# Batch 0 keeps 36 more score tiles and reads them back turned; queries, u and weight steps are placed anew

## The chip, the cores and the metric

One core of one Trainium2 chip. The metric is the device time of one execution in microseconds: the median of three runs, 2047.68 us for the kernel before (2046.53 to 2050.74). Engines: TensorE (PE) does the matmuls, VectorE (DVE), ScalarE (ACT) and GpSimd (POOL) work elementwise, SyncE (SP) issues the DMAs.

## What is computed

Two stages, in float32. Cut to what matters:

```python
# u, v: (4, 3008, 256); z: (4, 3008, 64)
scores = (1 / 3008) * z @ z.T              # per batch, symmetric
out = u * ((np.maximum(scores, 0) ** 2) @ v)
x = out.reshape(12032, 256)
xn = x / sqrt(mean(x * x, -1) + 1e-6) * rms_g
g, val = xn @ w_gate, xn @ w_val           # 256 -> 1536
y = (g * sigmoid(g) * val) @ w_out         # 1536 -> 256
```

The scores are symmetric: the score of query q and key k is that of query k and key q. The kernel uses this to compute some score tiles once and to read them back transposed.

## The kernel before

**Numbers.** Every float32 operand is split into a high and a low part for TensorE, and a product is three matmuls (high x high, low x high, high x low). A score needs two, since z stands in its array as high and low at once.

**Stages.** The 4 batches are cut into 3 pairs of query chunks (2 x 512 queries), so there are 12 pairs p, three for each batch. Each pair has an attention phase A(p) and a phase M(p) for the second stage. The attention phases of batch 0, p = 0, 1, 2, run first, one after the other (called phase 0, 1 and 2 here); then M(0), A(3), M(1), A(4) and so on. In the trace phase 0 ends at about 92 us, phase 1 at about 190 us, and the first matmuls of M(0) come at 276 us.

**A phase.** It has 24 slots, one for each tile of 128 keys, in the sequence that `order(p)` gives. In slot i the program writes: the scores of tile i + 2 for both query chunks (`emit_s`: two matmuls L415, L416 each; relu on ACT, L423; then either the product with itself on DVE, L430, or, for every second one, two squares on ACT, L450 and L451); the split of tile i + 1 into H on ACT (L453 or L450) and L on DVE (L456); a hook with whatever was planned for this slot; and the 12 matmuls of tile i with v (`emit_av`, L501, L502, L506). So a slot is 16 matmuls. At the end of a phase `emit_gate` multiplies the four sums by u (L531) and sends them to DRAM.

**Kept and turned tiles.** Where `keeps(b, c, kc)` says so, the tile of query chunk c and key chunk kc > c is also copied as 16-bit halves (`halves`, L475 on DVE or L477 on ACT, two of five on DVE; three buffers) and stored in DRAM (`kept`, L481). A later pair for which the chunks change places loads it with a transposing DMA (`load_turned`, L394), one load for two key tiles and one query chunk, into one of six buffers with the tag T. Such a slot needs no score matmuls, no relu and no product; H and L are made from the loaded tile. The later batches keep every such tile. Batch 0 keeps only those of chunk 4 against 5: four.

**Weights.** During phases 0, 1 and 2 the weights are decoded from 64-bit halves and combined: loads into the same six T buffers (`wraw`, L152), four short steps on DVE, one on ACT, then pieces of 128 columns on POOL (L140 for the projections, L201 and L202 for w_out). A combination is split by ACT (`wohi`, L231) and POOL (`wolo`) and stored in DRAM by SP (L236) one slot later. `at_step(g, ...)` places each at slot g % 24 of phase g // 24. The norm of pair 0 runs in slots 5 to 19 of phase 1 and in phase 2.

**Order.** The program's order is kept on each engine (`manual_schedule`): an engine runs its instructions as written and waits at each for what it needs. SP issues all DMAs in one order too, so a DMA that waits holds up those behind it. The queries of phases 1 and 2 (`prep_mov`, L292) go through the two buffers `raw`, which v, z and two of the four u tiles use as well; a split on DVE (L296, L301) makes mh and ml of them in slots 21 and 22 of the phase before. The u tiles are loaded (`load_u`, L521) in slots 21 (one) and 23 (three).

Of the kernel before, what the change touches and what calls it, by code (L numbers as in the profile page):

```python
# [8 lines left out]
F32 = mybir.dt.float32  # L9
# [21 lines left out]
def kernel(  # L31
# [176 lines left out]
    def prep_proj(j, pool, tags):  # L208
# [62 lines left out]
        "batch": ["mh0", "ml0", "mh1", "ml1", "raw", "raw"],  # L271
        "queries": ["raw"],
    }
# [7 lines left out]
    def prep_mov(p, k):  # L281
# [5 lines left out]
        def load():  # L287
            if p >= LAG:
                raw = tiles["raw"] = work.tile([P, CH], F32, tag=("u", "ws")[k], name="raw")
            else:  # L290
                raw = tiles["raw"] = new_raw("queries" if p else "start")
            nc.sync.dma_start(out=raw[:, :n], in_=zT2[:, t0 + k * CH:t0 + k * CH + n])  # L292
# [79 lines left out]
    def order(p):  # L372
        b, c0 = where(p)[:2]
        if p == 0:
            return list(range(NK))
        first = list(range(4 * (c0 + 1), min(4 * (c0 + 2), NK)))
        last = list(range(4 * c0, 4 * c0 + 4))
        return first + [k for k in range(NK) if k not in first and k not in last] + last

    def keeps(b, c, kc):  # L380
        return b > 0 or c >= 4

# [527 lines left out]
    for p in range(NPAIR):  # L910
# [4 lines left out]
        for i in range(0, NK, 2):  # L915
            for k in range(2):
                if is_turned(p, i, k):
                    go = lambda p=p, i=i, k=k: load_turned(p, i, k)
                    if i < 8 and p >= LAG:
                        at(("M", p - LAG), 3 * (NF - 2 if i < 6 else NF - 1) + 1, go)  # L920
                    else:
                        at(ph, max(i - 7, 0), go)
        if p >= LAG - 1:
            for f in range(ahead(p - LAG + 1)):
                at(ph, NK - 3 + f, lambda p=p, f=f: load_unit(p - LAG + 1, f))
        at(ph, NK - 3, lambda p=p: load_u(p, [(0, 0)]))
        at(ph, NK - 1, lambda p=p: load_u(p, [(0, 1), (1, 0), (1, 1)]))

# [73 lines left out]
    for p in range(1, NPAIR):  # L1002

        for k in range(2):
# [5 lines left out]
            else:  # L1010
                at(("A", p - 1), NK - (5 if p == 1 else 10), load)
                at(("A", p - 1), NK - 3 + k, split)
# [31 lines left out]

    for j, steps, end in ((0, (4, 8, 12, 16), 20), (1, (21, 25, 29, 33), 36), (2, (37, 40, 43, 47), 50)):
        parts, ends = prep_proj(j, moving, tags_w[j])
        for g, part in zip(steps, parts):
            plan_part(part, g)
        for k, fns in zip((0, 1, 2, 3, 5, 7, 8, 10, 12), ends):
            for fn in fns:  # L1050
                at_step(end + k, fn)
    for f, g in zip(range(0, 8, 2), (50, 55, 59, 63)):
        plan_part(prep_wout(f), g)
# [74 lines left out]
```

## Time and profile before

| | |
|---|---|
| median of 3 runs | 2047.68 us |
| the profiled execution, device time | 2047.41 us |
| its span, first to last instruction | 2045.6 us |
| PE busy | 2023.9 us (99%), 8976 matmuls |
| DVE, ACT, POOL busy | 1610.9, 1426.3, 225.8 us |
| granted TensorE clock, mean | 0.998 |

A matmul's busy time is modelled and its neighbours overlap, so a PE that is busy for 99% need not run at its best pace; how many matmuls a stretch holds says more. A short wait of PE and the lower clock after it show as fewer matmuls in a stretch. Rows of the trace name an engine, the line, the operation and the tiles (out<-in). A wait is put down to the instruction that ended it.

### The profile page before, as it was taken

The page shows a single profiled execution, that of the slowest core. Times are in us where ns is not written, and L with a number is a line of the kernel's source. Part 1 is how long each engine was busy: PE and PEld are TensorE (multiplying, and loading weights), DVE is VectorE, ACT ScalarE, POOL GpSimd, SP SyncE. Part 2 cuts the span into 40 slices and gives each one's busy share as a digit, 9 for nine tenths or more (in the row PEclk, how much of TensorE's full clock was granted, in tenths as well). Part 3 has the DMA queues.
Part 4 walks back from the last instruction along what each step waited for, and adds up shares of the span by engine and source line. Part 5 has one row for each costly group of instructions (what it writes and reads, how often), then busy time and mean ns, then how long its engine had stood idle before and what let it go on. Part 6 is the DMA issues. An engine that isn't in the chain of part 4 may idle for free.

```text
span 2045.6 us, 27209 instructions
## 1 busy us (share of the span) xinstructions
PE 2023.9 (99%) x8976; PEld 1680.8 (82%) x8976; DVE 1610.9 (79%) x2657; ACT 1426.3 (70%) x2578; POOL 225.8 (11%) x376
## 2 busy tenths in 40 slices
PE   9998999999999999999999999999999999999999
PEld 7786888888888888888888888888888888888887
DVE  7888988988877768797776876878777777777765
ACT  8787977886675666697567574679656757566665
POOL 0355815100000000400000000220000000000000
PEclk9999999999999999999999999999999999999999
DMA  3345375264555496346465459725544747734342
GB/s 110 108 125 160 108 240 183 104 211 148 134 157 183 141 212 213 103 163 210 136 144 173 147 147 203 234 89 174 196 134 128 212 136 169 190 126 157 118 147 91
DMA packets 320654, 320.50 MB, mean 157 GB/s; under 512 B 196736, under 2 KB 235776, under 8 KB 320512
## 3 DMA queue, kind: packets, MB, share of 16 engines
q1 hardware_dynamic: 320512, 318.77, 51.7%
q8 instruction: 70, 1.15, 0.2%
q14 instruction: 72, 0.59, 0.1%
HBM read 190.78 MB, written 81.79 MB: 133 GB/s over the span
## 4 chain that ended last, share of the span: by engine, by line
PE 88%; DVE 4%; ACT 3%; issue 2%; POOL 2%; DMA 1%; SPq 0%; DVEq 0%; ACTq 0%; POOLq 0%
PE po L501 11%; PE po L502 11%; PE po L506 11%; PE ps L700 10%; PE ps L701 10%; PE ps L702 10%; PE py L728 6%; PE py L729 6%; PE py L732 6%; PE ps L416 4%; PE ps L415 4%; POOL w L140 1%; POOL wolo L140 1%; ACT s L707 1%; ACT r L423 1%
## 5 line engine op out<-in xcount | busy, mean ns | idle before, releaser
L501 PE MATMUL po<-H,vh 128*128 128x512 f32 (+1 forms) x1152 | 447.8, 389 | 4.5 <-DVE u L531 2.1
L502 PE MATMUL po<-H,vl 128*128 128x512 f32 (+1 forms) x1152 | 445.4, 387 | 0.0
L707 ACT COPY s<-ps 128x512 f32<-128x512 f32 (+1 forms) x432 | 249.5, 578 | 217.5 <-PE ps L702 217.5
L700 PE MATMUL ps<-xh,wu 128*128 128x512 f32 (+1 forms) x1008 | 392.0, 389 | 1.9 <-ACT s L707 1.8
L701 PE MATMUL ps<-xh,wu 128*128 128x512 f32 (+1 forms) x1008 | 388.7, 386 | 0.0
L702 PE MATMUL ps<-xl,wu 128*128 128x512 f32 (+1 forms) x1008 | 388.6, 385 | 0.0
L506 PE MATMUL po<-L,vh 128*128 128x512 f32 (+1 forms) x1104 | 336.8, 386 | 3.5 <-DVE L L456 3.0
L712 ACT CAST hH<-s 128x512 fp32r<-128x512 f32 (+1 forms) x288 | 176.6, 613 | 203.9 <-DVE s L794 200.1
L430 DVE TENSOR_TENSOR r<-ps,r 128x512 f32<-128x512 f32 (+1 forms) x327 | 213.9, 681 | 99.7 <-ACT r L423 98.7
L423 ACT ACTIVATE r<-ps 128x512 f32<-128x512 f32 (+1 forms) x392 | 214.8, 593 | 110.1 <-PE ps L416 96.0
L717 DVE TENSOR_TENSOR hL<-s,hH 128x512 fp32r<-128x512 f32 (+1 forms) x288 | 201.0, 698 | 104.4 <-ACT hH L712 91.1
L501 PEld LDWEIGHTS po<-H,vh 128*128 128x128 f32 x1152 | 216.8, 188 | 52.7 <-DVE H L460 2.7
L456 DVE TENSOR_TENSOR L<-r,H 128x512 fp32r<-128x512 f32 x368 | 248.0, 706 | 14.4 <-ACT r L451 14.3
L502 PEld LDWEIGHTS po<-H,vl 128*128 128x128 f32 x1152 | 217.0, 188 | 40.5
L506 PEld LDWEIGHTS po<-L,vh 128*128 128x128 f32 x1104 | 206.7, 188 | 46.1 <-DVE L L456 7.4
L700 PEld LDWEIGHTS ps<-xh,wu 128*128 128x128 f32 x1008 | 189.1, 188 | 47.0 <-ACT s L707 10.0
L728 PE MATMUL py<-hH,woh 128*128 128x512 f32 (+1 forms) x576 | 222.2, 386 | 0.1
L729 PE MATMUL py<-hH,wol 128*128 128x512 f32 (+1 forms) x576 | 222.0, 385 | 0.0
L702 PEld LDWEIGHTS ps<-xl,wu 128*128 128x128 f32 x1008 | 189.2, 188 | 36.1
L701 PEld LDWEIGHTS ps<-xh,wu 128*128 128x128 f32 x1008 | 189.2, 188 | 34.9 <-DMA wu<-wc 0.4
L453 ACT CAST H<-r 128x512 fp32r<-128x512 f32 (+1 forms) x327 | 191.5, 622 | 3.3 <-DVE r L430 3.2
L362 POOL TENSOR_TENSOR vl<-raw,vh 128x128 fp32r<-128x128 f32 x144 | 81.4, 603 | 940.2 <-ACT vh L351 937.6
(85 smaller groups left out, 2912.4 us busy)
## 6 DMA issues: line engine op xcount, KB each, us to landing
wu<-wc SPq DMA_DIRECT2D x288, 448.0 KB, 4.0
kept<-halves SPq DMA_DIRECT2D x168, 256.0 KB, 2.0
raw<-in_v SPq DMA_DIRECT2D x44, 256.0 KB, 2.9
u<-in_uT SPq DMA_DIRECT2D x40, 256.0 KB, 4.6
xg<-u SPq DMA_DIRECT2D x40, 256.0 KB, 2.3
raw<-in_zT SPq DMA_DIRECT2D x38, 256.0 KB, 4.5
ux<-xg SPq DMA_DIRECT2D x16, 512.0 KB, 4.8
out_T<-y SPq DMA_DIRECT2D x32, 256.0 KB, 2.2
```

The lines of the kernel that those rows point to most:

```text
L423: nc.scalar.activation(a[:, :n], ps[:, :n], AF.Relu)
L430: nc.vector.tensor_tensor(a[:, :n], ps[:, :n], a[:, :n], op=ALU.mult)
L456: nc.vector.tensor_tensor(lo[:, :n], a[:, :n], f32(hi[:, :n]), op=ALU.subtract)
L501: nc.tensor.matmul(po[d][:, :n], wh[:, j, ds], hi[:, :n], start=(i == 0), stop=False)
L502: nc.tensor.matmul(po[d][:, :n], wl[:, j, ds], hi[:, :n], start=False, stop=(ends and lo is None))
L506: nc.tensor.matmul(po[d][:, :n], wh[:, j, ds], lo[:, :n], start=False, stop=ends)
L700: nc.tensor.matmul(ps[:, :n], wh[:, o, :], xh[:, :n], start=start, stop=False, skip_group_check=True)
L701: nc.tensor.matmul(ps[:, :n], wl[:, o, :], xh[:, :n], start=False, stop=False, skip_group_check=True)
L702: nc.tensor.matmul(ps[:, :n], wh[:, o, :], xl[:, :n], start=False, stop=stop, skip_group_check=True)
L707: nc.scalar.copy(s, ps[:, :self.n])
L728: nc.tensor.matmul(acc[h, d][:, :n], woh[:, f, ds], hi[:, :n], start=(f == 0), stop=False)
L729: nc.tensor.matmul(acc[h, d][:, :n], wol[:, f, ds], hi[:, :n], start=False, stop=False)
```

## The change

It does six things. (1) `keeps` lets batch 0 keep more: chunk 0 against 2 and 3, chunk 1 against 4 and 5, chunks 2 and 3 against every later one, 36 tiles more (16 made in phase 0, 20 in phase 1; 12 read in phase 1, 24 in phase 2). (2) In batch 0 `order` takes new and turned key tiles by turns, two and two. (3) Turned tiles of the first phases are loaded five slots ahead, not seven. (4) The queries of phases 1 and 2 go to buffers of their own, q0 and q1, and those of phase 1 are loaded in slot 14, not 19, of phase 0. (5) In every phase the u tiles are loaded two in slot 21 and two in slot 22. (6) The steps of the second and third part of the projection weights and of w_out get other numbers.

```diff
@@ -269,7 +269,6 @@
     raws = {
         "start": ["raw", "xl4", "raw", "xl5", "xl6"],
         "batch": ["mh0", "ml0", "mh1", "ml1", "raw", "raw"],
-        "queries": ["raw"],
     }
 
     def new_raw(what):
@@ -285,10 +284,11 @@
         tiles = {}
 
         def load():
-            if p >= LAG:
-                raw = tiles["raw"] = work.tile([P, CH], F32, tag=("u", "ws")[k], name="raw")
+            if p:
+                tag = ("u", "ws")[k] if p >= LAG else f"q{k}"
+                raw = tiles["raw"] = work.tile([P, CH], F32, tag=tag, name="raw")
             else:
-                raw = tiles["raw"] = new_raw("queries" if p else "start")
+                raw = tiles["raw"] = new_raw("start")
             nc.sync.dma_start(out=raw[:, :n], in_=zT2[:, t0 + k * CH:t0 + k * CH + n])
 
         def high():
@@ -375,10 +375,20 @@
             return list(range(NK))
         first = list(range(4 * (c0 + 1), min(4 * (c0 + 2), NK)))
         last = list(range(4 * c0, 4 * c0 + 4))
-        return first + [k for k in range(NK) if k not in first and k not in last] + last
+        rest = [k for k in range(NK) if k not in first and k not in last]
+        if b == 0:
+
+            new, old = [], []
+            for k in rest:
+                (old if k // 4 < c0 and keeps(b, k // 4, c0) else new).append(k)
+            rest = []
+            while new or old:
+                rest += new[:2] + old[:2]
+                del new[:2], old[:2]
+        return first + rest + last
 
     def keeps(b, c, kc):
-        return b > 0 or c >= 4
+        return b > 0 or c >= 2 or kc // 2 == c + 1
 
     def is_turned(p, i, k):
         b, c0 = where(p)[:2]
@@ -919,12 +929,12 @@
                     if i < 8 and p >= LAG:
                         at(("M", p - LAG), 3 * (NF - 2 if i < 6 else NF - 1) + 1, go)
                     else:
-                        at(ph, max(i - 7, 0), go)
+                        at(ph, max(i - (7 if p >= LAG else 5), 0), go)
         if p >= LAG - 1:
             for f in range(ahead(p - LAG + 1)):
                 at(ph, NK - 3 + f, lambda p=p, f=f: load_unit(p - LAG + 1, f))
-        at(ph, NK - 3, lambda p=p: load_u(p, [(0, 0)]))
-        at(ph, NK - 1, lambda p=p: load_u(p, [(0, 1), (1, 0), (1, 1)]))
+        at(ph, NK - 3, lambda p=p: load_u(p, [(0, 0), (0, 1)]))
+        at(ph, NK - 2, lambda p=p: load_u(p, [(1, 0), (1, 1)]))
 
     def plan_splits(p, phase, slots):
         jobs_ = split_jobs_at(p)
@@ -1008,7 +1018,7 @@
                 at(m.phase, 3 * 9 + 1 + k, load)
                 at(m.phase, 3 * 10 + 2 + k, split)
             else:
-                at(("A", p - 1), NK - (5 if p == 1 else 10), load)
+                at(("A", p - 1), NK - 10, load)
                 at(("A", p - 1), NK - 3 + k, split)
 
 
@@ -1042,14 +1052,14 @@
         for k, (_, _, _, fn) in zip((0, 0, 0, 1, 1, 2, 2, 2), ops):
             at_step(g + k, fn)
 
-    for j, steps, end in ((0, (4, 8, 12, 16), 20), (1, (21, 25, 29, 33), 36), (2, (37, 40, 43, 47), 50)):
+    for j, steps, end in ((0, (4, 8, 12, 16), 20), (1, (18, 26, 29, 33), 36), (2, (36, 39, 42, 50), 52)):
         parts, ends = prep_proj(j, moving, tags_w[j])
         for g, part in zip(steps, parts):
             plan_part(part, g)
         for k, fns in zip((0, 1, 2, 3, 5, 7, 8, 10, 12), ends):
             for fn in fns:
                 at_step(end + k, fn)
-    for f, g in zip(range(0, 8, 2), (50, 55, 59, 63)):
+    for f, g in zip(range(0, 8, 2), (53, 56, 60, 64)):
         plan_part(prep_wout(f), g)
 
     with tc.manual_schedule():
```

What this does to the order on three engines' queues follows.

SP at the end of phase 0; raw<-in_zT of L292 are the queries, u the u tiles, wc the combined weights. Before:

```order
L152 DMA wraw<-in_w_gate 128x1024
L292 DMA raw<-in_zT 128x512 x2
L521 DMA u<-in_uT 128x512
L236 DMA wc_80<-wohi 128x4x128
L236 DMA wc_80<-wolo 128x4x128
L152 DMA wraw<-in_w_gate 128x1024
L236 DMA wc_80<-wohi 128x4x128
L236 DMA wc_80<-wolo 128x4x128
L521 DMA u<-in_uT 128x512 x3
```

After:

```order
L292 DMA raw<-in_zT 128x512 x2
L491 DMA kept_804<-halves 128x1024
L343 DMA raw<-in_v 128x2x256
L152 DMA wraw<-in_w_gate 128x1024
L491 DMA kept_804<-halves 128x1024 x2
L345 DMA raw<-in_v 128x256
L347 DMA raw<-in_v 64x256 x2
L491 DMA kept_804<-halves 128x1024
L491 DMA kept_982<-halves 128x1024 x3
L531 DMA u<-in_uT 128x512 x2
L236 DMA wc_80<-wohi 128x4x128
L236 DMA wc_80<-wolo 128x4x128
```

The queries now stand ahead of the last loads of v, and two u tiles ahead of the first weight store; stores of kept tiles have come in between.

ACT in phase 1 at slots 15 and 16 (L433 is the relu, L463 and L460 make H, L461 squares, L487 copies the halves). Before:

```order
L423 ACTIVATE r<-ps 128x512 x2
L453 CAST H<-r 128x512
L450 ACTIVATE H<-r 128x512
L451 ACTIVATE r<-r 128x512
L423 ACTIVATE r<-ps 128x512 x2
L450 ACTIVATE H<-r 128x512
L451 ACTIVATE r<-r 128x512
L453 CAST H<-r 128x512
L157 ACTIVATE w_1846<-wraw 128x512
```

After:

```order
L433 ACTIVATE r<-ps 128x512 x2
L463 CAST H<-r 128x512
L460 ACTIVATE H<-r 128x512
L461 ACTIVATE r<-r 128x512
L487 COPY halves<-r 128x1024 x2
L157 ACTIVATE w_1873<-wraw 128x512
L433 ACTIVATE r<-ps 128x512 x2
L460 ACTIVATE H<-r 128x512
L461 ACTIVATE r<-r 128x512
L463 CAST H<-r 128x512
L487 COPY halves<-r 128x1024
```

Each slot has got one or two copies of twice the width behind its tiles.

SP in the second half of phase 2 (T<-kept are the transposing loads, wraw<-in_w_out the last weights). Before:

```order
L152 DMA wraw<-in_w_out 128x2x512
L236 DMA wc_82<-wohi 128x4x128
L236 DMA wc_82<-wolo 128x4x128
L236 DMA wc_82<-wohi 128x4x128
L236 DMA wc_82<-wolo 128x4x128
L152 DMA wraw<-in_w_out 128x2x512
L236 DMA wc_82<-wohi 128x4x128
L236 DMA wc_82<-wolo 128x4x128
L394 DMA_TRANSPOSE T<-kept_2184 128x2x896
L236 DMA wc_82<-wohi 128x4x128
L236 DMA wc_82<-wolo 128x4x128
L394 DMA_TRANSPOSE T<-kept_2184 128x2x896
```

After:

```order
L404 DMA_TRANSPOSE T<-kept_1654 128x2x1024
L404 DMA_TRANSPOSE T<-kept_1855 128x2x896
L404 DMA_TRANSPOSE T<-kept_1654 128x2x1024
L404 DMA_TRANSPOSE T<-kept_1855 128x2x896
L152 DMA wraw<-in_w_out 128x2x512
L236 DMA wc_82<-wohi 128x4x128
L236 DMA wc_82<-wolo 128x4x128
L404 DMA_TRANSPOSE T<-kept_1657 128x2x1024
L404 DMA_TRANSPOSE T<-kept_1858 128x2x896
L236 DMA wc_82<-wohi 128x4x128
L236 DMA wc_82<-wolo 128x4x128
L236 DMA wc_82<-wohi 128x4x128
```

Pairs of transposing loads now stand among the stores of wolo, which wait for POOL, and share the T buffers with the loads of w_out.

## Rows read from the trace of the kernel before

**Rows 1.** Stretches (us): PE, PEld, DVE, ACT, POOL busy (count), clock, DMA share, GB/s

```profile
25.00:87.00 62.00, 62.00 (x275) 51.32 (x275) 51.90 (x85) 54.82 (x102) 11.63 (x20) 1.00 0.22 70
87.00:105.00 18.00, 15.36 (x58) 11.53 (x57) 17.10 (x27) 11.12 (x21) 10.62 (x16) 0.91 0.67 214
105.00:168.00 63.00, 63.00 (x280) 52.20 (x279) 54.32 (x84) 55.91 (x104) 37.60 (x63) 1.00 0.42 127
168.00:203.00 35.00, 27.38 (x107) 20.43 (x107) 30.47 (x53) 22.50 (x41) 20.64 (x34) 0.95 0.54 162
203.00:262.00 59.00, 58.30 (x264) 48.82 (x263) 55.72 (x80) 53.98 (x103) 49.22 (x73) 1.00 0.42 115
276.00:2045.00 1769.00, 1762.22 (x7853) 1467.94 (x7852) 1370.99 (x2284) 1196.47 (x2153) 90.03 (x160) 1.00 0.54 161
```

**Rows 2.** Waits of PE, 0 to 260 us: total us, times, longest

```profile
PE ps L415 <- DVE mh L296: 4.4, 3, 2.1
PE po L506 <- DVE L L456: 3.0, 4, 1.3
PE po L501 <- DVE u L531: 2.1, 2, 1.6
```

**Rows 3.** Time line of SP: start, us, line, operation, tiles, count

```profile
73.73 13.90 SPq L292 DMA_DIRECT2D raw<-in_zT  x2
...
192.72 0.36 SPq L236 DMA_DIRECT2D wc<-wolo  x1
193.18 1.43 SPq L521 DMA_DIRECT2D u<-in_uT  x3
```

**Rows 4.** Waits of SP's queue, 0 to 260 us: total us, times, longest

```profile
SPq L236 <- POOL wolo L140: 62.7, 21, 7.7
...
SPq L292 <- DVE vl L357: 25.3, 2, 13.1
```

**Rows 5.** DMA issues: count, KB each, median us to landing

```profile
u<-in_uT SPq DMA_DIRECT2D x40, 256.0 KB, 4.6
...
T<-kept SPq DMA_TRANSPOSE x92, 4.8
```

**Rows 6.** Groups of ACT, 25 to 75 us: busy us, mean ns, idle before

```profile
L423 ACT ACTIVATE r<-ps 128x512 f32<-128x512 f32 x28 | 15.2, 594 | 4.3 <-PE ps L416 4.3
...
L453 ACT CAST H<-r 128x512 fp32r<-128x512 f32 x14 | 8.6, 614 | 0.0
```

**Rows 7.** The copies of kept tiles, whole run: ns min/median/max

```profile
L477 ACT COPY halves<-r x118: 1028/1056/1093, 195.1 to 1716.9; 128x1024 uint16<-128x1024 uint16 x102, 64x1024 uint16<-64x1024 uint16 x16
L475 DVE COPY halves<-r x66: 684/690/698, 377.9 to 1602.7; 128x1024 uint16<-128x1024 uint16 x66
```

**Rows 8.** Stretches with POOL nearly idle and full, columns as in rows 1

```profile
25.00:75.00 50.00, 50.00 (x222) 41.38 (x222) 41.32 (x68) 45.28 (x85) 7.46 (x12) 1.00 0.26 82
216.00:260.00 44.00, 43.30 (x195) 35.83 (x194) 43.00 (x61) 39.13 (x76) 42.73 (x61) 1.00 0.44 119
```

**Rows 9.** DVE's L and product in those two stretches: ns min/median/max

```profile
L456 DVE TENSOR_TENSOR L<-r,H x26: 681/686/804, 27.4 to 71.5; 128x512 fp32r<-128x512 f32 x26
L456 DVE TENSOR_TENSOR L<-r,H x26: 667/838/1020, 216.7 to 259.6; 128x512 fp32r<-128x512 f32 x13, 128x448 fp32r<-128x448 f32 x13
L430 DVE TENSOR_TENSOR r<-ps,r x14: 682/684/693, 25.7 to 74.7; 128x512 f32<-128x512 f32 x14
L430 DVE TENSOR_TENSOR r<-ps,r x13: 611/648/679, 216.1 to 257.5; 128x512 f32<-128x512 f32 x7, 128x448 f32<-128x448 f32 x6
```

**Rows 10.** SP's issues of transposing loads, whole run: ns min/median/max

```profile
L394 SPq DMA_TRANSPOSE T<-kept x92: 1311/2100/5577, 252.7 to 1749.8; - x92
```

## The prediction

> **What bounds the kernel now.** I read the table of stages first [rows 1]. From 276 us to the end TensorE holds 7853 matmuls in 1769 us and stands still for under 7 us, so nothing is to be had there. Batch 0's first phase is as dense: 275 matmuls in 62.00 us, 0.2255 us each, with ACT busy 54.82 and DVE 51.90. What is open lies around the phases' ends. At 0.2255 us the stretch 87 to 105 us has room for 79.8 matmuls and holds 58: 4.9 us lost. The stretch 168 to 203 us has room for 155.2 and holds 107: 10.9 us lost. From 203 to 262 us there are 264, half of them 448 columns wide (0.028 us shorter): 59.0 - 264 x 0.2255 + 132 x 0.028 = 3.2 us lost. Together 19.0 us. The clock shows in two of them: 0.91 over 18 us and 0.95 over 35 us are 3.2 and 3.5 us at the lower of the two levels (1.2 GHz), after TensorE had stood still; at half pace that is 1.6 and 1.8 us of the losses.
>
> The waits of TensorE name the releasers [rows 2]: the scaled queries mh of the next phase (4.4 us), L of a tile (3.0), the gate on u (2.1). The queue of SP says why they are late [rows 3]. The queries' two loads span 13.90 us, since the second waits for a buffer; three u loads stand behind a store of wolo that goes out at 192.72, once POOL has the data. SP's own waits have both: 13.1 us at most for the buffer, 7.7 for POOL [rows 4].
>
> **The change, part by part.**
>
> *Score matmuls.* 36 tiles fewer to multiply (12 in phase 1, 24 in phase 2), two matmuls each: 24 and 48, of which 24 are 448 wide. 48 x 0.2255 + 24 x 0.2255 x 448/512 = 15.6 us less on TensorE, and TensorE is what runs through [rows 1]. Gain 15.6.
>
> *Queries and u.* The queries get q0 and q1, free in phase 0 and, in phase 1, after the reduction at slot 12; they are issued at slot 14, some 7 slots before their split. Nothing there waits for raw. The u loads move ahead by a slot or two and, at the end of phase 1, ahead of the last wolo store of that phase. A u load lands in 4.6 us [rows 5], well within the two slots of 3.6 us (16 matmuls) that are left. I take 1.0 us as what is left of the 4.9 (0 to 3, what DVE's own queue may still cost the split): gain 3.9.
>
> *Kept copies, first phase.* 36 new copies, 18 on ACT (1.056 us) and 18 on DVE (0.690) [rows 7]. Phase 0 has 10 of ACT's and 7 of DVE's (one belongs to the next phase's first tile). 10 x 1.056 = 10.6 us come to a stretch in which ACT is idle for 62.0 - 54.8 = 7.2 us [rows 1], of which 6.2 lie behind the first copy (at 34 us, slot 7). ACT's instructions run into one another: 85 take 45.28 us, 0.533 each [rows 8], while a relu alone has 0.594 and an H 0.614 [rows 6]. At that ratio a copy costs 0.92, and the excess is 3.0 to 4.4 us. Some of it goes into the lead that ACT has. I take a cost of 2.0 (0 to 4.4). DVE's 7 x 0.69 = 4.8 fit into its 10.1 idle us.
>
> *Kept copies, second phase.* In slots 11 to 18 of phase 1 two tiles a slot are kept. ACT has there 15 relu, 24 H and square forms and 6 weight steps, 45 x 0.533 = 24.0 us, and 9 copies at 0.92 to 1.056: 32.3 to 33.5 us, against 127 matmuls = 28.6. Excess 3.7 to 4.9. The same stretch is where DVE, with the norm's short steps and the weights, costs most of the 10.9 us: DVE is busy 30.47 of 35 while TensorE stands still [rows 1]. More time per slot for ACT is more time for DVE too, so the two don't add in full. I put 5 us (3 to 9: the smaller excess less some lead; the larger with some four of today's own) for the slots and 2 us (0 to 4) for the phase's end, where u is no longer late but the split still stands in DVE's queue: 7 in place of 10.9, gain 3.9 (from a gain of 7.9 to a loss of 2.1).
>
> *Turned tiles in place of new ones, third phase.* Here slots shrink from 16 matmuls to 12, while POOL's weight work stays: 4 pieces of the fourth weight, 44 of the combinations, 32 of w_out, starting at slot 4. POOL is the full engine there already: 42.73 of 44 us, 61 pieces, 0.700 us each [rows 8]; over 105 to 168 us it was 63 pieces in 37.60 us, 0.597 each [rows 1]. SP's order now puts transposes behind stores that wait for POOL, and the six T buffers turn round: the pair for tile 16 takes a buffer that w_out's second piece leaves when POOL has done 44 pieces, the one for tile 20 the buffer of the third, at 68. A transpose holds SP for 1.3 to 2.1 us and lands in 4.8 [rows 5, 10]; then H (0.614) and L (0.838 while POOL is full) follow [rows 6, 9]. Tile 16: 26.3 to 30.8 us of POOL, 3.4 for two issues, 4.8, 1.5 make 36.0 to 40.5 us after slot 4; TensorE is there after 152 matmuls x 0.221 (58.30 us over 264 [rows 1]) = 33.6 us. Tile 20: 40.6 to 47.6, 2.1, 4.8, 1.5 make 49.0 to 56.0, against 204 x 0.221 = 45.1. So 3.9 to 10.9 us late in all, 1 more for POOL's start behind the decode and 1 for what the slots before still lose. I take 8 (4 to 13): between the two paces, since DVE does fewer products. Against the 3.2 of today a cost of 4.8 (0.8 to 9.8).
>
> A rule that speaks against this part bears on POOL's pace. The rows: L of a tile (two operands in SBUF) has a median of 686 ns while POOL is nearly idle and 838 ns while it is full, though half of the latter are narrower; the product from PSUM goes from 684 to 648, that is with its width [rows 8, 9]. The Trainium skill, "SBUF — State Buffer", "Who interferes with whom", says that a DVE instruction with two SBUF inputs and a GpSimd one that reads SBUF exclude each other, and that one with a single SBUF input does not contend. The trace agrees. By that rule the change takes away the products, which were no hindrance, and leaves every L, now closer together: POOL would get no faster. That is the second rival.
>
> *At nothing:* the removed relu, squares and products (36, 34 and 19 instructions; 17 plain H casts come in) free ACT and DVE in slots where TensorE is the bound; the weights' new steps keep their number; for the later batches only u moves by a slot, and TensorE doesn't wait there [rows 1]. Of what SP gets more, the 18 transposes weigh most, 18 x 2.1 = 38 us of issuing in 190 [rows 10].
>
> **Sum.** -15.6 - 3.9 + 2.0 - 3.9 + 4.8 = -16.6 us. The profiled span of 2045.6 becomes 2029.0. Around the span lie 1.8 us (2047.41 against 2045.6), so 2030.8 for such an execution; the median of the runs is 0.3 above it: 2031.
>
> **The rivals.**
> *POOL sets the third phase at 0.700 us a piece.* For it: the row of the full POOL [rows 8]. The rule above would have it so. Against: 0.597 in the phase before, with DVE nearly as busy (54.32 of 63). It loses 12.9 us in place of 8: -11.7, 2036.
> *The copies are hidden and the ends are clean.* ACT's excess goes into its lead in both phases, POOL keeps 0.6: -15.6 - 4.9 + 0 - 7.9 + 0.8 = -27.6, 2020. For it: TensorE lost nothing from 105 to 168 us with ACT at 89% [rows 1].
> *The gain is eaten.* All bounds at their bad end: -15.6 - 1.9 + 4.4 + 2.1 + 9.8 = -1.2, about 2046; the same comes out if the relieved TensorE only waits for ACT and DVE, the change thus not doing what it says.
> *SP is held and the transposes come late, slower.* A pair needs 2 x 2.1 + 4.8 = 9.0 us, and is issued five slots ahead, 60 matmuls or 13.3 us; it stands 4.3 us of delay. There are eight new pairs. If SP is held behind a POOL store for 7.7 us, the longest of its kind [rows 4], at each of them, 8 x 3.4 = 27 us come to the -16.6: 2058. It turns slower from 6.4 us held at every pair. Against: only about five pairs stand right behind such a store.
>
> **How the numbers follow.** The forecast, 2025 to 2034 around 2031: 0.52. POOL at 0.700: 0.22. All hidden: 0.17. Eaten, within 0.2% (4.1 us, about what runs of this kernel can tell apart): 0.05. Slower: 0.04. Faster is 0.52 + 0.22 + 0.17 = 0.91, same 0.05, slower 0.04. Range 2020 to 2041: it takes in the clean case and, above POOL's, half the way to the eaten one.
>
> **What would show it.** Right: 72 fewer score matmuls; 87 to 105 us with 70 matmuls or more and no wait of the first query product over 1 us; u gates without a DMA wait; ACT above 95% busy in the late second phase and TensorE waiting there for H or L in steps under 1.5 us; in the third phase waits of 2 us or more at tiles 16 and 20, with POOL full and SP waiting on POOL. Wrong: a third phase without such waits (POOL faster than 0.6 a piece), TensorE waiting from 30 us on (ACT's excess was too small), or a stretch of low clock in the third phase, which would add what the two today cost, 1.6 to 1.8 us each.

## The result, and the profile after

The changed kernel takes 2064.07 us, the median of 4 runs (2062.35 to 2064.72), against 2047.59 for the kernel before, run beside it: 1.0077 times, interval 1.0064 to 1.0089. It is slower, by 16.5 us. The forecast was 2031, the range 2020 to 2041. The profiled span is 2062.6 us.

The 72 matmuls are gone (8904 against 8976). The first product of M(0) comes at 290.8 us all the same, not at 276.0. The stretches of the changed kernel, columns as in [rows 1]:

```profile
25.00:87.00 62.00, 61.09 (x267) 49.57 (x267) 53.26 (x88) 59.62 (x108) 10.64 (x17) 1.00 0.38 127
87.00:105.00 18.00, 13.66 (x47) 9.63 (x46) 15.94 (x24) 9.45 (x17) 12.75 (x20) 0.86 0.54 166
105.00:168.00 63.00, 60.70 (x262) 48.68 (x260) 54.14 (x81) 55.41 (x97) 34.81 (x55) 0.99 0.77 221
168.00:203.00 35.00, 28.21 (x100) 19.97 (x99) 29.55 (x51) 22.10 (x40) 23.67 (x38) 0.90 0.77 213
203.00:291.00 88.00, 73.75 (x306) 59.18 (x304) 68.71 (x101) 55.17 (x103) 54.32 (x84) 0.94 0.83 209
291.00:2062.00 1771.00, 1763.00 (x7852) 1467.34 (x7850) 1371.96 (x2287) 1195.37 (x2150) 89.43 (x160) 1.00 0.53 161
```

Every stretch ahead of M(0) holds fewer matmuls than before, the quiet ones (25 to 87, 105 to 168) too. The DMA engines' share in 105 to 168 us is 0.77, not 0.42. With the prediction's measure (room at 0.2255 us a matmul, 0.028 less for 448 columns) the losses of TensorE are:

| stretch | lost before, us | lost after, us | what the prediction left, us |
|---|---|---|---|
| 25 to 87 | 0 | 1.8 | 2.0 |
| 87 to 105 | 4.9 | 7.4 | 1.0 |
| 105 to 168 | 0 | 3.9 | 0 |
| 168 to 203 | 10.9 | 12.4 | 7 |
| third phase (203 to 276; 203 to 291) | 3.6 | 23 | 8 |

That is 29 us more lost, against 15.6 of removed work. Part of it is the clock. Reckoned as the prediction does (time at the lower level goes at half pace), the granted clocks of the rows give an estimate of 3.4 us lost to it before and of some 12 after: 2.5 in 87 to 105 us, 0.6 in 105 to 168, 3.5 in 168 to 203 and 5.3 in the third phase. From M(0) on the program takes some 2 us longer.

The waits of TensorE in the first 292 us (total us, times, longest; the answer to [rows 2]):

```profile
PE po L511 <- ACT H L463: 11.1, 6, 4.7
PE po L516 <- DVE L L466: 9.1, 14, 1.4
PE ps L425 <- DVE mh L296: 4.4, 2, 2.7
PE po L511 <- DVE H L470: 2.9, 2, 2.3
```

The gate on u is gone from the list. The wait for mh is what it was, 4.4 us, though the second chunk's queries now land at 72.6 us, not at 89.9. New are H of ACT and many small waits for L. SP's queue in the same stretch (the answer to [rows 4]) now waits for the copies:

```profile
SPq L491 <- DVE halves L485: 50.5, 12, 17.2
SPq L236 <- POOL wolo L140: 33.0, 14, 6.0
SPq L491 <- ACT halves L487: 25.0, 17, 3.2
...
SPq L404 <- POOL wol L202: 9.5, 2, 5.0
```

Its time line at the end of the first phase (the answer to [rows 3]) shows what that does to the u loads:

```profile
82.32 10.67 SPq L491 DMA_DIRECT2D kept<-halves  x4
93.04 0.93 SPq L531 DMA_DIRECT2D u<-in_uT  x2
94.07 0.38 SPq L236 DMA_DIRECT2D wc<-wohi  x1
98.34 0.38 SPq L236 DMA_DIRECT2D wc<-wolo  x1
99.75 0.52 SPq L491 DMA_DIRECT2D kept<-halves  x1
100.34 1.05 SPq L531 DMA_DIRECT2D u<-in_uT  x2
```

Four stores that wait for their copies stand ahead of the first two u loads, and a store of wolo and a fifth copy ahead of the last two: at this end the loads are planned earlier and issued no earlier. At the end of the second phase all four go out at 190.2 us, and no gate waits for a load any more. Before, DVE waited there for one:

```profile
DVE u L531 <- DMA u<-in_uT: 3.7, 1, 3.7
```

### The profile page after: what moved, and what is told of

Read it like the earlier page. It is cut to its first block, busy times and chain, and to the rows that moved or that the text cites. A ratio compares the mean times of both kernels' runs of the same rounds, so it can differ in the third digit from the quotient of the medians.

```text
span 2062.6 us, 27118 instructions
## 1 busy us (share of the span) xinstructions
PE 2023.8 (98%) x8904; PEld 1672.2 (81%) x8904; DVE 1609.6 (78%) x2656; ACT 1416.4 (69%) x2543; POOL 225.8 (11%) x376
## 4 chain that ended last, share of the span: by engine, by line
PE 82%; ACT 6%; DVE 5%; DMA 3%; issue 2%; POOL 1%; SPq 0%; ACTq 0%; DVEq 0%; POOLq 0%
PE po L511 10%; PE ps L710 10%; PE po L512 10%; PE ps L711 10%; PE ps L712 10%; PE po L516 10%; PE py L738 5%; PE py L739 5%; PE py L742 5%; PE ps L426 3%; PE ps L425 3%; ACT r L433 1%; DVE L L466 1%; ACT halves L487 1%; ACT H L463 1%
## 5 line engine op out<-in xcount | busy, mean ns | idle before, releaser
L440 DVE TENSOR_TENSOR r<-ps,r 128x512 f32<-128x512 f32 (+1 forms) x308 | 201.2, 680 | 101.2 <-ACT r L433 101.0
L433 ACT ACTIVATE r<-ps 128x512 f32<-128x512 f32 x356 | 196.1, 594 | 103.1 <-PE ps L426 91.5
L466 DVE TENSOR_TENSOR L<-r,H 128x512 fp32r<-128x512 f32 x332 | 219.5, 691 | 13.9 <-ACT r L461 12.9
L463 ACT CAST H<-r 128x512 fp32r<-128x512 f32 (+1 forms) x308 | 180.1, 622 | 3.4 <-DVE r L440 3.4
```

Source lines behind the costliest of these rows:

```text
L433: nc.scalar.activation(a[:, :n], ps[:, :n], AF.Relu)
L440: nc.vector.tensor_tensor(a[:, :n], ps[:, :n], a[:, :n], op=ALU.mult)
L466: nc.vector.tensor_tensor(lo[:, :n], a[:, :n], f32(hi[:, :n]), op=ALU.subtract)
```

## The experiments

Each time is the median of its runs; the ratio is against the kernel before, run beside it, with its 95% interval. Theories: **P**, the new places cost; **C**, the copies and their stores cost; **S**, in the third phase SP holds loads behind POOL and the T buffers; **D**, the transposing loads cost by themselves; **V**, DVE's time is the bound.

### The places: e1_place, e2_keep, e10_queries_u

The change was cut in two. e1 has the places (queries, u, weight steps) and no further tile; e2 the tiles, the key order and the lead, with the old places; e10 queries and u alone:

```diff
 e1, against the changed kernel (and the old order and lead)
-        return b > 0 or c >= 2 or kc // 2 == c + 1
+        return b > 0 or c >= 4
 e10, also
-(1, (18, 26, 29, 33), 36), (2, (36, 39, 42, 50), 52)):   ...   (53, 56, 60, 64)
+(1, (21, 25, 29, 33), 36), (2, (37, 40, 43, 47), 50)):   ...   (50, 55, 59, 63)
```

> The kernel before with the new places alone (queries in q0 and q1, u two slots at a time, new weight and w_out steps); no further tile kept, old key order. If the new places are what costs (theory P), the two phase ends that lose 5.4 and 11.8 us in the kernel before lose more and the time is above 2052. If the kept tiles cost (theories C, S and D), the places by themselves do what the prediction said of them: 3 to 9 us off, 2039 to 2045.

> The changed kernel with the old places of queries, u, weights and w_out: the kept tiles, the key order and the shorter lead alone. Theory P (places cost): under 2055. Theories C, S and D (kept tiles cost): 2064 to 2075, since what the places give is gone too.

> The kernel before with the new places of queries and u alone; weights, w_out, kept tiles as before. The placement as a whole gave 4.8 us at the end of the second phase and took 5.5 in the third. If the later weight and w_out steps did both (less of DVE's work in the second phase, more in the third), this one is at the time of before, 2047 to 2049. If queries and u gave the 4.8 us and the steps took the 5.5, it is 2042 to 2045.

Measured: e1 2049.75 us (1.0005, 0.9996 to 1.0014), e2 2063.07 (1.0067, 1.0052 to 1.0082), e10 2046.71 (0.9990, 0.9981 to 0.9999). So P falls as the cause of the loss, and the places are worth about nothing as a whole: with them or without, the tiles bring the time to 2063 or 2064. The 3 to 9 us that e1 was expected to win did not come. Two stretches of e1 show why (columns as above):

```profile
168.00:203.00 35.00, 30.91 (x131) 23.62 (x130) 29.26 (x49) 25.25 (x47) 19.81 (x33) 1.00 0.49 158
203.00:276.00 73.00, 68.60 (x302) 55.30 (x301) 67.24 (x101) 61.77 (x118) 54.44 (x80) 1.00 0.45 127
```

At the end of the second phase e1 has 131 matmuls where the kernel before has 107 [rows 1], 5.4 us won. In the third it has 302 where that has 328, over 5 us lost: the weights' work was only moved there. e10, without the new steps, has 121 matmuls in 168 to 203 us and 58 in 87 to 105, there as many as before. So 3.2 of the 5.4 us come from queries and u; but M(0) begins only 0.9 us earlier (275.1 against 276.0), and over the whole run they give 1 to 2 us, not the 4.8 that e10 was to test.

### The copies: e3_no_readback, e6_no_copy, e7_copy_pool

e3 copies and stores the 36 tiles but multiplies their scores anew. e6 does the same without the copies. e7 gives the first phase's copies to POOL:

```diff
 e3
-        return kc < c0 + k and keeps(b, kc, c0 + k)
+        return kc < c0 + k and (b > 0 or kc >= 4)
 e6, also (no copy for these tiles)
+  part = a[:m].bitcast(U16).rearrange("p (h q) -> p h q", h=2) if whole else halves[:m]
 e7, against the changed kernel
+                if p == 0:
+                    nc.gpsimd.tensor_copy(halves[:m], split)
```

> The changed kernel, in which the 36 new tiles are copied and stored but not loaded back: their scores are multiplied anew (72 matmuls more, 15.6 us of TensorE). Theory C (the copies on ACT and DVE and their stores cost the 30 us that TensorE loses more before the second stage begins): 2064 + 15.6 = 2080. Theories S and D (the transposing loads cost, by SP's queue or by the DMA engines' load): the 30 us go, 2064 + 15.6 - 30 = 2050. By the stretches of the two traces, 19 of the 30 us lie in the third phase, which only loads: 2060.

> As e3_no_readback (36 tiles stored, none of them loaded back, scores multiplied anew), but without the copies: the stores take the float32 tile as it stands, so what they write isn't halves and nothing reads it. Against e3 (2063.7) and the placement alone (2049.8): theory C1 (ACT's and DVE's time for the copies is the 14 us): 2050 to 2054. Theory C2 (the stores in SP's order and in the DMA engines are): 2060 to 2064.

> The changed kernel with the 16 new copies of the first phase on POOL instead of ACT and DVE. Theory C1: the first phase and its end lose 5 us less (2.3 + 9.3 against 1.1 + 5.4 without copies), 2058 to 2061. If POOL holds DVE off while it copies, or takes over 3.6 us for a copy and so delays the weights: 2065 and more.

Measured: e3 2063.66 us (1.0072, 1.0055 to 1.0089), e6 2053.85 (1.0029, 1.0017 to 1.0041), e7 2071.54 (1.0119, 1.0102 to 1.0135). This gives a chain: places alone 2049.75; 4.1 more with the stores (e6, which has the new key order too); 9.8 more with the copies (e3); and then 72 matmuls less and the reading back, 0.4 more (the changed kernel), which is within the noise. Reading back costs about the 15.6 us that it saves. Of e6's 4.1 us only 1.7 lie ahead of M(0), which begins at 277.6 us, against 275.9 in e1; the rest falls behind it.

So the copies are a large part, C1 of the expectations (the engines' time, not the stores). SP's queue could still be the way by which they cost, since its stores wait for them; but from 25 to 203 us TensorE waits in e3 for DVE and ACT alone, never for a load. Where it loses, three stretches of e6 and then of e3 show:

```profile
25.00:87.00 62.00, 62.00 (x275) 51.32 (x275) 53.11 (x87) 55.42 (x103) 12.82 (x20) 1.00 0.41 133
...
105.00:168.00 63.00, 63.00 (x281) 52.12 (x280) 55.30 (x87) 55.75 (x103) 35.80 (x61) 1.00 0.61 202
168.00:203.00 35.00, 30.99 (x130) 23.55 (x129) 29.94 (x52) 25.09 (x46) 21.42 (x36) 1.00 0.55 173
```

```profile
25.00:87.00 62.00, 61.07 (x267) 49.59 (x266) 53.53 (x88) 59.61 (x108) 11.27 (x18) 1.00 0.38 124
...
105.00:168.00 63.00, 62.09 (x271) 49.93 (x270) 54.88 (x83) 60.51 (x107) 34.52 (x58) 1.00 0.59 192
168.00:203.00 35.00, 28.63 (x104) 21.18 (x105) 30.93 (x54) 24.39 (x44) 22.35 (x35) 0.90 0.56 172
```

From 25 to 203 us e3 has 45 matmuls less than e6; 26 of them are missing in 168 to 203 us, where the last tiles that come two to a slot are copied (until 182 us in the changed kernel) and the norm runs on DVE. The changed kernel there, first ACT's full stretch, then DVE's:

```profile
165.00:172.00 7.00, 6.30 (x26) 4.46 (x26) 4.69 (x8) 6.94 (x12) 5.69 (x11) 1.00 1.04 301
172.00:181.00 9.00, 6.41 (x27) 4.57 (x27) 8.24 (x19) 7.81 (x14) 3.15 (x6) 1.00 0.93 237
```

ACT is busy for 6.94 of 7 us, then DVE for 8.24 of 9: it looks as if what one engine delays the other inherits, but no run takes the two apart. POOL is no way out: a copy takes it 1.4 us, and L on DVE beside it 816 ns in the mean, against 694 in the changed kernel (groups of e7, 25 to 90 us on POOL and 25 to 75 us on DVE):

```profile
L485 POOL COPY halves<-r 128x1024 uint16<-128x1024 uint16 x14 | 19.3, 1399 | 12.2 <-issue 6.8 <-ACT r L461 5.4
```

```profile
L466 DVE TENSOR_TENSOR L<-r,H 128x512 fp32r<-128x512 f32 x26 | 20.2, 816 | 3.4 <-ACT r L461 3.4
```

### The reading back: e4_plain, e5_wout_dve, e9_no_decode, e11_wout_early, e8_wout_m0, e12_m0_dve

What TensorE waits for in the third phase of the changed kernel, 203 to 291 us, 14.1 us in all:

```profile
PE po L511 <- ACT H L463: 10.0, 5, 4.7
PE po L516 <- DVE L L466: 3.6, 5, 1.1
PE po L511 <- DVE H L470: 0.5, 1, 0.5
```

Two of these waits are long, 3.3 and 4.7 us, both for H of ACT (rows of the time line; the wait stands in brackets):

```profile
256.82 0.80 PE L511 MATMUL po<-H,vh 128*128 128x512 f32 x1 [3.31 <-ACT H L463]
...
274.88 0.80 PE L511 MATMUL po<-H,vh 128*128 128x512 f32 x1 [4.66 <-ACT H L463]
```

They stand ahead of tiles 14 and 18, and the granted clock is low after them, 0.72 from 256 to 262 us and 0.50 from 274 to 280. Behind the first, one matmul starts 0.43 us after another, elsewhere 0.23. What ACT waits for between 250 and 276 us, and what SP waits for:

```profile
ACT woh L157 <- DMA wraw<-in_w_out: 7.8, 2, 5.5
ACT wohi L231 <- POOL w L140: 4.9, 1, 4.9
ACT H L463 <- DMA T<-kept: 2.2, 2, 1.1
```

```profile
SPq L404 <- POOL wol L202: 5.0, 1, 5.0
SPq L404 <- POOL wolo L140: 3.1, 1, 3.1
```

It is not the turned tile that is late. The load of w_out's next part stands in SP's order behind a transposing load that waits for a T buffer of POOL's; ACT and DVE reach that part in their own order and stand, with H and L of tiles that have landed behind it. Ahead of the second long wait this is all: ACT stands for 5.5 us at the load and makes H right behind it. Ahead of the first it stands for 4.9 us at POOL's w and then for 2.4 at the load. Six runs take single pieces of this away:

```diff
 e4: t filled by plain loads of v in place of the transposing one
 e5: w_out's last steps on DVE in whole tiles, not in POOL's pieces
+                nc.vector.tensor_tensor(f32(wh), f32(wh), f32(hi), op=ALU.subtract)
+                nc.vector.tensor_tensor(lo, f32(wh), f32(wl), op=ALU.add)
 e9: DVE's decode steps left out from step 50 on
+            if e == "a" or k == 2 and fn is ops[-1][3] or g < 50:
 e11: w_out's loads at g - 6, not g - 3
 e8: two of the four parts in M(0)
-    for f, h in zip(range(8, NF, 2), (9, 15)):
+    for f, h in zip(range(4, NF, 2), (2, 8, 14, 20)):
 e12: e8 and e5 together, in M(0) too
```

> The changed kernel, in which each of the 18 new transposing loads is replaced by two plain loads of the same bytes from v (so the attention of batch 0 is computed from other numbers). All waits for T buffers and for SP's neighbours stay. Theory D (a transposing load's issue of 2.1 us and over and its small packets are what costs): most of the third phase's 19 us goes, 2045 to 2050. Theory S (the loads stand in SP behind POOL and the T buffers, whatever their kind): 2 to 5 us go, 2059 to 2062. Theory C: 2064.

> The changed kernel with the 64 POOL pieces of w_out's first four parts (third phase) done as 8 whole-tile operations on DVE. Theory S (POOL's row of pieces keeps the T buffers, SP holds the transposes and the next w_out load behind it, ACT and DVE stand at that load in their own order): most of the two waits of 3.5 and 4.8 us and the low clock after them go, 2050 to 2056. Theory V (in the third phase DVE itself is the bound, its L taking 0.945 us beside POOL): the 8 operations are 5.5 us more for DVE, so 2062 to 2068.

> The changed kernel without the 25 decoding operations of DVE for the last five weight parts of the third phase (16.7 us of DVE's 63.1 there); their loads bring the same number of bytes from v, and ACT's and POOL's steps stay, so these weights are wrong. Theory V (DVE's time bounds the third phase): it gives back 10 us or more, 2050 to 2054. Theory S (ACT stands at the late loads and SP at POOL's pieces): 0 to 4 us, 2060 to 2064.

> The changed kernel with w_out's four loads of the third phase issued six slots ahead of their first step, not three, so in SP's order ahead of the transposing loads that wait for POOL. Theory S: ACT's and DVE's waits for these loads (7.8 us each) go, and 4 to 8 us with them, 2056 to 2060. If the T buffers are what is short, the transposing loads are late instead: 2062 to 2068. Theory V: within 2 us of 2064.

> The changed kernel with two of w_out's four parts taken out of the third phase and made in M(0) instead, ahead of the two that are made there already. Theory S: a third or more of the third phase's 19 us goes, since the late loads are the third and the fourth: 2052 to 2057. Theory D (the transposing loads themselves): 2062 to 2064.

> As e8_wout_m0, with w_out's POOL pieces done by DVE in whole tiles, in the third phase and in M(0). In e8 the third phase lost 8 us less and M(0) 11 us more. If M(0) lost them because its weight loads share the T buffers, which POOL's pieces held, they go: 2053 to 2057. If DVE in M(0) has no room for them either, 2062 and more.

| run | time, us | ratio (interval) | first product of M(0), us |
|---|---|---|---|
| changed kernel | 2064.07 | 1.0077 (1.0064 to 1.0089) | 290.8 |
| e4, plain loads | 2059.01 | 1.0049 (1.0034 to 1.0064) | 283.7 |
| e5, w_out on DVE | 2061.42 | 1.0072 (1.0057 to 1.0087) | 287.4 |
| e9, no decode | 2057.50 | 1.0042 (1.0027 to 1.0057) | 281.7 |
| e11, w_out early | 2062.30 | 1.0070 (1.0055 to 1.0085) | 286.3 |
| e8, half in M(0) | 2066.42 | 1.0094 (1.0079 to 1.0109) | 284.2 |
| e12, e8 on DVE | 2065.29 | 1.0087 (1.0070 to 1.0104) | 280.1 |

No theory has it alone. D: the loads' kind is worth 5.1 us, over the second and the third phase (the edit takes the two old transposing loads of batch 0 too). V: 16.7 us of DVE's work left out give 6.6, and not all of that need be DVE's time, since its own waits at the late loads and ACT's for the decode go with it. What is left in e9 is S, with DVE busy for 54.11 of 79 us:

```profile
ACT woh L161 <- DMA wraw<-in_v: 10.1, 3, 6.3
```

S: with the loads issued early (e11), ACT's wait for w_out is gone and another has its place:

```profile
ACT H L463 <- DMA T<-kept: 13.8, 6, 5.5
```

So the six T buffers, POOL and DVE seem to be one chain, in which whoever goes first makes the other late; no run gives the phase more buffers. e8 and e12 take half of w_out out of the phase. M(0) begins 6.6 and 10.7 us earlier, and both are not faster in the end: M(0) gives it back. SP in e12:

```profile
327.95 0.42 SPq L152 DMA_DIRECT2D wraw<-in_w_out  x1
339.14 3.66 SPq L347 DMA_DIRECT2D raw<-in_v  x2
342.89 0.89 SPq L698 DMA_DIRECT2D wu<-wc  x2
```

The planner of M(0) counts the new steps against DVE's room and so places batch 1's loads and splits anew; a load of v now waits 10.7 us for its buffer, M(0)'s own weights (wu) stand behind it, and TensorE waits 4.0 us for them at once.

### The count, one part of w_out, and DVE's queue at the phase ends: e14_counter, e16_wout_one, e15_split, e17_split_counter

```diff
 e14, on the changed kernel
+                n_before = copies[0] - (36 if b else 0)
+                if c0 <= 2 and n_before % 5 in (1, 3):
 e15, on e10 (e17: on e14)
-                at(("A", p - 1), NK - 3 + k, split)
+                at(("A", p - 1), NK - 3, split)
 e16, on e10: parts at steps 50, 55, 60 and, in M(0), slots 2, 9, 15
```

> The changed kernel, in which the count that sends two of five copies to DVE starts again where it stood in the kernel before when batch 1 begins (36 new copies shift it by one). From the first matmul of M(0) to the end the kernel before has 1769.6 us, those with 36 more copies 1771.8 to 1775. If the shifted count is the cause, this stretch falls to 1769.5 to 1771 and the time by 1 to 4 us, 2060 to 2063. If the late start of M(0)'s weight loads is the cause, it stays at 2064.

> e10_queries_u with one of w_out's four parts of the third phase made in M(0) instead, in slots ahead of the two that are made there, the other steps of M(0) left where they are. The third phase loses 5.7 us in e10. If relief there is a gain that M(0) can take, 2043 to 2045; if M(0)'s weight loads are delayed by it as in e8 and e12, 2047 to 2052.

> e10_queries_u (new places of queries and u alone, 2046.7) with the split of the second query chunk in the same slot as that of the first, ahead of L of the phase's last tile and of the weights' decode on DVE. If the first score of the next phase waits for DVE's queue and not for the queries' load, the waits of 2.3 and 1.8 us at 93 and 188 us and the low clock after them go: 2041 to 2044. If the split only changes places with L of the last tiles, which TensorE needs as well, 2046 to 2049.

> The changed kernel with both the count of e14 and the split of e15. If the ends of the first two phases hang on DVE's queue, the waits for mh of 3.0 and 2.0 us go: 4 to 6 us below e14, 2055 to 2058. If DVE is so far behind there that L of the last tiles takes their place, 2060 to 2063.

Measured: e14 2063.93 us (1.0080, 1.0065 to 1.0095), no change; from M(0) on it has 1772.6 us, so the shifted count is not what makes that part longer. e16 2047.27 (0.9998, 0.9988 to 1.0007), against e10's 2046.71 nothing won: M(0) begins 1.2 us earlier (273.9 against 275.1), and the rest takes 1.6 us longer.

e15 2044.01 (0.9984, 0.9975 to 0.9993), e17 2060.17 (1.0062, 1.0047 to 1.0077): 2.7 us under e10 and 3.8 under e14 (by the ratios 1.2 and 3.7, and the intervals of each pair overlap). DVE at the end of the first phase in e10, where TensorE waits for mh from 93.7 us on:

```profile
93.47 1.70 DVE L460 TENSOR_TENSOR H<-r,H 64x512 fp32r<-64x512 f32 x2
95.20 0.57 DVE L296 TENSOR_SCALAR mh<-raw 128x512 fp32r<-128x512 f32 x1
95.80 0.83 DVE L301 SCALAR_TENSOR_TENSOR ml<-raw,mh 128x512 fp32r<-128x512 f32 x1
```

DVE works without a gap: the split of the second chunk stands behind the last tile's operation, with its queries long there. Put ahead of it, it leaves TensorE waiting for that operation instead, 1.7 us in e15:

```profile
PE po L501 <- DVE H L460: 1.7, 1, 1.7
```

The order was worth some 1 to 4 us, the queue itself remains.

### A smaller set of tiles: e18_keep_c0, e19_keep_late

```diff
 on e15, with the changed kernel's key order and lead
-        return b > 0 or c >= 4
+        return b > 0 or c >= 4 or c == 0 and kc // 2 == 1      (e18, 8 tiles more)
+        return b > 0 or c >= 2                                 (e19, 20 tiles more)
```

> e15_split (2044.0) with 8 more tiles kept, not 36: chunk 0 against 2 and 3, copied in the first phase and read in the second, where POOL isn't full; key order and lead as in the changed kernel. TensorE does 16 matmuls less, 3.6 us. If a copy costs what it cost in e3 against e6 (10 us for 36) and the reading back little in the second phase: 2.2 us for copies, 2042 to 2044. If each tile costs in reading what the 36 did (about 16 us), nothing is left: 2045 to 2048.

> e15_split with 20 more tiles kept, all copied in the second phase (chunk 2 against 3, 4, 5 and chunk 3 against 4, 5), 4 of them read there and 16 in the third. 40 matmuls less, 9.0 us at most. If the loss goes with the number of copies and loads (20 of 36 of some 30 us is 17): 2050 to 2054. If the first phase's copies were the dear ones and these are hidden: 2040 to 2046.

Measured: e18 2042.74 us (0.9977, 0.9968 to 0.9986), e19 2045.62 (0.9990, 0.9981 to 0.9998). e18 is the fastest kernel of this study, 5.1 us under the kernel before; e15 alone has 4.0 of these, and between the two the intervals overlap. The first 8 tiles give some 1.3 of 3.6 us, if anything: in the profiled runs e18 reaches M(0) 2.3 us before e15 (268.9 against 271.2 us) and takes 1.9 us longer from there on. The 20 late ones lose some 1.6 to e15, again with overlapping intervals, while TensorE has 9.0 us less to do. The stretch 168 to 203 us has 131 matmuls in e15 and in e18, 116 in e19, and M(0) begins 2.4 us later than in e15: it is the copies at the second phase's end, and the reading in the third, that don't pay.

## Why the prediction was wrong, by its own steps

**The step that failed first** is the term for the third phase: a loss of 8 us (4 to 13) was put there, and it was 23. The two long waits that it is made of did come, at tiles 14 and 18 in place of 16 and 20, and with 8.0 us together they have the size forecast (3.9 to 10.9). That the size fits is in part luck: it was to be the turned tile that comes late, and it was a weight step in ACT's own order. What the sum left out is the rest: 6.1 us of shorter waits, where it had 1 us for what the slots still lose, and the low clock after the waits, some 5 us by the estimate above, which it had at nothing. At the prediction's own pace of 0.221 us, 306 matmuls are 67.6 us; with 14.1 us of waits and the 5.3 of the clock that makes 87 of the 88.

**Score matmuls, a gain of 15.6: done, but taken back.** 72 are gone. The sum let each one count in full, "and TensorE is what runs through", with rows of M(0) and later behind it. In the third phase of the kernel before that was nearly a tie, DVE being busy for 69.70 of 73 us, beside TensorE's 72.30:

```profile
203.00:276.00 73.00, 72.30 (x328) 60.90 (x327) 69.70 (x102) 65.88 (x125) 55.04 (x81) 1.00 0.48 139
```

24 tiles fewer there take about 12 products from DVE, 8 us at 0.65, not the 24 turned tiles' L, while slots shrink from 16 matmuls to 12. The relief of DVE was put at nothing, "in slots where TensorE is the bound", and whether DVE keeps up with the shorter slots was not asked. From 240 to 250 us it is busy for 9.86 of 10, and TensorE waits for L. How much of the gain DVE took isn't shown: over the whole phase it is busy for 68.71 of 88 us, and without 16.7 us of its work (e9) 6.6 come back.

**Queries and u, a gain of 3.9: none at the first phase's end.** The reason was mistaken. The late loads of [rows 3] were real, but covered by DVE's queue, which reached the split no earlier: with the queries there by 72.6 us TensorE waits 2.7 us for mh, and e10 has the same 58 matmuls in 87 to 105 us as the kernel before. The bound of 0 to 3 us "what DVE's own queue may still cost" named it, and the value taken, 1.0, was too small. In e15 the order on DVE gives 1 to 3 us, with the loads as in e10. And u's new place was undone at this end by the stores of the copies ahead of it on SP, a queue that the prediction passed over in this step. At the second phase's end u did what was forecast: the wait of 3.7 us for its load is gone.

**Copies of the first phase, a cost of 2.0 (0 to 4.4): right.** 275 matmuls against 267 from 25 to 87 us are 1.8 us; e3 against e6 has the same 8. Over both phases the new copies are 21 on ACT and 15 on DVE, not 18 each as the prediction says; its sum doesn't use these two numbers.

**The second phase, a gain of 3.9 (down to a loss of 2.1): a loss of some 5.** Lost are 3.9 us in 105 to 168, which the sum had at nothing, and 12.4 in 168 to 203, not 7, of which the low clock (0.90) is some 3.5. e3 against e6 gives the size: 36 matmuls or 8.1 us by copies alone over the two stretches, while the new places give 5.4 there (e1). ACT's excess (3.7 to 4.9 us) is part of it. That DVE's time follows ACT's and isn't covered by it, against "the two don't add in full", is how the rows at 165 and 172 us read; no run shows it by itself.

**The third phase, more closely.** The mechanism was right as far as SP, wrong at the end. SP does wait for POOL's wol, 5.0 us, and a piece of POOL takes 0.65 us (54.32 for 84), between the forecast's two paces. But the turned tiles cost ACT 2.2 us of waiting; the load of w_out behind them cost it 7.8, and in this the prediction missed that a weight step stands in ACT's and DVE's order as a transfer does in SP's. Into the same term belong over 5 us that the new places brought there (e1, most of it by the weights' new steps, since e10 loses only some 1 us more there than the kernel before; "the weights' new steps keep their number" was put at nothing) and the transposing loads' kind (5 us, e4, with the second phase's), which hold SP for 2.3 us in the median and up to 3.7, not 1.3 to 2.1.

**The rivals.** The fourth came nearest, 2058 at a chance of 0.04: SP held, slower. Its price was right in kind, but it had the loss at eight pairs of tiles and not in copies, DVE and w_out. The third has a clause that fits as well, that "the relieved TensorE only waits for ACT and DVE", at a chance of 0.05 and with no loss. POOL's 0.65 us a piece isn't the 0.700 of the second.

**What would show it.** No wait of TensorE from 30 us on: right, the first after that comes at 63.1. No gate waiting for a load of u: right. 70 matmuls in 87 to 105 us: 47, and 2.7 us of waiting for mh, not under 1. ACT above 95% late in the second phase: 6.94 of 7 us at 165, then not. Waits of 2 us or more in the third phase: right, at tiles 14 and 18. Low clock in the third phase: 0.94 over 88 us, named as a sign of being wrong, and it was.

**Open.** From M(0) on the kernels that keep the 36 tiles take 1772 to 1776 us (e8 and e12 1783), those with the old set 1769.6 to 1772. e14 rules out the count; M(0)'s weight loads are at hand late (TensorE waits 0.7 us for wu), but that was not tried by itself. How the third phase's 16 us divide between buffers, DVE and transposes can't be added up from e4 to e12, since each piece taken away uncovers the next.

## What to carry to other kernels

Before counting removed matmuls as time, read DVE, ACT and POOL in that very stretch: where one of them is nearly as busy as TensorE, as DVE was here (69.70 beside 72.30 us), ask what the change takes from that engine too. Work that is moved to keep a tile (copy, store, turned load) has to be put on each engine's queue and each shared buffer, and the weights' steps with it: each engine here runs its instructions in order, so a step that waits for a late load (5.5 us on ACT) holds everything behind it. A wait also costs the lower clock after it, which belongs in the sum. Try the smallest set first: here 8 tiles cost nothing and may give 1.3 us, while 36 made the kernel 14 us slower than the places alone.

## What the runs showed of the hardware that was not expected

**POOL and DVE slow each other.** L of a tile takes 683 ns in the median while POOL is nearly idle and 883 beside its full row (25 to 75 and 236 to 263 us; min/median/max):

```profile
L466 DVE TENSOR_TENSOR L<-r,H x27: 679/683/829, 24.7 to 74.1; 128x512 fp32r<-128x512 f32 x27
...
L466 DVE TENSOR_TENSOR L<-T,H x13: 816/883/948, 240.8 to 262.6; 128x512 fp32r<-128x512 f32 x7, 128x448 fp32r<-128x448 f32 x6
```

That the second row reads T is not the reason: from 460 to 635 us, with POOL idle, L from T takes 684 in the median. And POOL's piece is short when DVE stands. The four pieces of the second row here run from 271.9 to 273.5 us, while DVE waits for a load; the others of 244 to 276 us run beside it:

```profile
L140 POOL TENSOR_TENSOR wolo<-w,wohi 128x128 fp32r<-128x128 f32 x16 | 11.8, 772 | 0.0
...
L140 POOL TENSOR_TENSOR wolo<-ws,wohi 128x128 fp32r<-128x128 f32 x4 | 1.7, 453 | 0.0
```

So a piece moved between the two is not simply moved; with w_out's pieces on DVE (e5) M(0) began only 3.4 us earlier. The Trainium skill, "SBUF — State Buffer", "Who interferes with whom", has a DVE instruction with two SBUF inputs and a GpSimd one that reads SBUF contend; these rows agree, and e7's copies on POOL, which lengthen L by 122 ns, do too.

**A transposing load is not as cheap as a plain one here.** SP is held for 2.3 us in the median by each, up to 3.7, where a plain half takes 0.4 (e4), and the time was 5.1 us shorter with twice as many plain loads of the same bytes (e4). The Trainium skill, "Advanced Engine Details and Errata", "X-Bar Transpose (TRN2)", says that such transfers are as fast as regular ones. As to landing the trace agrees nearly (4.8 us, against 3.3 and 4.5 for plain halves in the third phase of e4); the time on the queue that issues them is another matter, on which the runs show the difference above.
